# Loading a 2 KB vector in 16 descriptors and spreading it with selecting products, beside a stream of large loads

## The chip, the cores and the metric

The kernel runs on one core of one Trainium2 chip. The metric is the time of one execution on the device in microseconds (us), as the median of several executions. The profile is of a single execution; its span, from the first to the last instruction, is about 1.4 us shorter than the time.

## The reference

One token of decoding. A layer norm of x (1024 values) feeds two branches, whose results are added to x:

```python
x = A_x
xn = _layernorm(x, axis=-1)
return x + _A_ref(xn, A_k_cache, A_v_cache, A_wq, A_wo) + _B_ref(xn, B_w1, B_w2, B_w3, B_w4)
```

Branch A is attention of 32 query heads over 4 heads of K and V with 65,536 cached rows of 128. Branch B is a small network of two gelu layers with the weights w1 to w4. Everything is bf16. The weights are 36 MB and the cache is 134 MB, and each byte is read once: 169.87 MB for 2 KB of output.

## The kernel before

Three large SBUF slots take turns with 8.39 MB each (64 KB in each of 128 partitions): wq, then w1 with w2, then w3, then the eight K blocks (slots 0 and 2) and the eight V blocks (slot 1), then wo and w4. SP issues all of these. x alone is issued by ACT:

```python
_dma(q_act, chan("x"), lambda e: e.dma_start(out=x_bf, in_=A_x[0, 0, :].rearrange("(p j) -> p j", p=P)), writes=[b_x])
kv_load(0, "s0", rows_src(A_wq, 0, 8), 8 * HQD)
...  # w1, w2
kv_load(2, "s2", rows_src(B_w3, 0, 8), 8 * F)
```

A load is issued when its slot has been used up. For the first blocks this ties the loads to the front chain, which starts with x:

```python
_op(q_dve, lambda e: e.tensor_copy(xT, x_bf), reads=[b_x], writes=[b_xT])
...
layer_norm(xT, b_xT, xn, xn_bf, b_xn, 200)
...  # 64 products of xn with wq (slot 0)
issue(3)                                   # K0 into slot 0
...  # w1, w2
issue(4)                                   # V0 into slot 1
...  # w3, gelu -> gh_bf
q_sp.wait_all([(q.sem, q.cnt) for q in (q_pe, q_dve, q_act, q_pool)])
issue(5)                                   # K1 into slot 2
```

After each block m follow `issue(6 + 2 * m)` and `issue(7 + 2 * m)`, the next V and the K after the next. I call the loads K0, V0, K1, V1 and so on. The first instruction of SP and of ACT is moved to the head of the program, ahead of the start-up barrier.

Of the kernel before, what the change touches and what calls it, by code (L numbers as in the profile page):

```python
# [6 lines left out]
BF = mybir.dt.bfloat16  # L7
F32 = mybir.dt.float32
ACTF = mybir.ActivationFunctionType
ALU = mybir.AluOpType  # L10
# [89 lines left out]
def _deps(q, reads, writes):  # L100
    evs = [e for b in reads for e in b.w.items()]
    for b in writes:
        evs += list(b.w.items()) + list(b.r.items())
    q.wait_all(evs, in_order=q.name == "pe")


def _done(ev, reads, writes, partial=False):
    for b in reads:
        b.add_read(ev)
    for b in writes:  # L110
        if partial:
            b.add_write(ev)
        else:
            b.set_write(ev)


def _op(q, fn, reads=(), writes=(), partial=False, loop=False):
    _deps(q, reads, writes)
    ev = q.op(fn, True, loop)
    _done(ev, reads, writes, partial)  # L120
    return ev


def _grp(q, fns, reads=(), writes=(), partial=False):
    _deps(q, reads, writes)
    ev = None
    for i, fn in enumerate(fns):
        ev = q.op(fn, i == len(fns) - 1)
    _done(ev, reads, writes, partial)
    return ev  # L130
# [8 lines left out]
def _dma(q, chan, fn, reads=(), writes=(), partial=False):  # L139
    _deps(q, reads, writes)  # L140
    chan.n += 1
    ev = q.dma(fn, chan.sem, 16 * chan.n)
    _done(ev, reads, writes, partial)
    return ev


def bass_parallel_sum__gqa_block_cached__mixer_s_mlp__decode_kernel(
# [13 lines left out]
    P = 128  # L161
# [6 lines left out]
    KT_D = D // P  # L168
# [10 lines left out]
    with ExitStack() as es:  # L179
        E = es.enter_context  # L180

        def sb(name, shape, dt):
            return E(nc.sbuf_tensor(name, shape, dt))

        def ps(name, shape, dt):
            return E(nc.psum_tensor(name, shape, dt))

        def sem(name):
            return E(nc.semaphore(name))
# [5 lines left out]
        permR = sb("permR", [P, P], BF)  # L195
# [29 lines left out]
        def early(n, dt):  # L225
            size = n * (2 if dt is F32 else 1)
            o = e_off[0]
            e_off[0] = o + (size + 15) // 16 * 16
            assert e_off[0] <= SLOT
            v = KV[:, 2, o:o + size]  # L230
            return v.bitcast(F32) if dt is F32 else v
# [6 lines left out]
        maskA = early(4 * G, F32).rearrange("p (a g) -> p a g", a=4)  # L238
        mD32 = early(32 * 4, BF).rearrange("p (k a) -> p k a", a=4)
        neghalf = early(1, F32)  # L240
        permWE = early(4 * P, BF).rearrange("p (w q) -> p w q", w=4)
        x_bf = early(KT_D, BF)
        xT = early(KT_D, F32)
        xn = early(KT_D, F32)
        xn_bf = early(KT_D, BF)
# [9 lines left out]
        g_bf = early(KT_D, BF)  # L255
# [8 lines left out]
        M_ps = ps("M_ps", [P, 512], F32)  # L264

        _Q.clocks = {}
        q_pe = _Q("pe", sem("c_pe"))
        q_dve = _Q("dve", sem("c_dve"), sem("l_dve"))
        q_act = _Q("act", sem("c_act"), sem("l_act"))
# [4 lines left out]
        def chan(name):  # L274
            if name not in chans:
                chans[name] = _DmaChan(sem("d_" + name))
            return chans[name]

        b_const = _B()
        b_x = _B(); b_xT = _B(); b_xn = _B(); b_xn2 = _B(); b_qT = _B(); b_Y = _B(); b_Yc = _B()  # L280
# [8 lines left out]
        def kv_load(s, ch, src, n, bufs=None):  # L289
            _dma(q_sp, chan(ch), lambda e: e.dma_start(out=KV[:, s, 0:n], in_=src), writes=b_KV[s] if bufs is None else bufs)  # L290

        def rows_src(w, r0, nrow):
            return w.rearrange("(p r) n -> p (r n)", p=P)[:, r0 * w.shape[1]:(r0 + nrow) * w.shape[1]]

        _dma(q_act, chan("x"), lambda e: e.dma_start(out=x_bf, in_=A_x[0, 0, :].rearrange("(p j) -> p j", p=P)), writes=[b_x])
        kv_load(0, "s0", rows_src(A_wq, 0, 8), 8 * HQD)
        b_w1 = b_KV[1][0:2]
        b_w2 = b_KV[1][2:4]
# [15 lines left out]

        evs = []
        for t_, val in ((ident_bf, 0.0), (ident_f[:], 0.0), (ones_f, 1.0), (sel16[:], 1.0), (selGT_bf[0:8, :], 1.0), (selTT[0:4, :], 1.0),
                        (neghalf, -0.5), (permWE, 1.0), (permR[:], 1.0), (maskA, 1.0), (mD32, 1.0), (g_bf, 0.0)):
            evs.append(q_pool.op(lambda e, t_=t_, val=val: e.memset(t_, val)))
        q_pool.wait_all([evs[-1]])

        def sel(t_, pattern, op, base, mult, fill):
            return q_pool.op(lambda e: e.affine_select(out=t_, in_=t_, pattern=pattern, compare_op=op, fill=fill, base=base, channel_multiplier=mult))
# [4 lines left out]
        q_pool.wait_all([ev])  # L327
        sel(sel16[:], [[8, 16]], ALU.is_ge, 7, -1, 0.0)
        sel(selGT_bf[0:8, :], [[0, 16], [-1, 8]], ALU.is_equal, 0, 1, 0.0)
        sel(selTT[0:4, :], [[0, 4], [-1, 4], [0, 8]], ALU.is_equal, 0, 1, 0.0)  # L330
        sel(permWE, [[-64, 2], [-1, 2], [0, 4], [-2, 32]], ALU.is_equal, 0, 1, 0.0)
        sel(permR[:], [[-8, 4], [-32, 4], [-1, 8]], ALU.is_equal, 0, 1, 0.0)
# [3 lines left out]
        ev = sel(maskA, [[32, 4], [0, 8]], ALU.is_ge, 31, -1, 0.0)  # L336
        b_const.set_write(ev)

        _op(q_dve, lambda e: e.tensor_copy(xT, x_bf), reads=[b_x], writes=[b_xT])  # L339

        def layer_norm(src, b_src, dst_f, dst_bf, b_dst, c0):
            _op(q_dve, lambda e: e.reduce_sum(ln_s[:, 0:1], src, axis=AX.X), reads=[b_src], writes=[b_ln])
            _op(q_pe, lambda e: e.matmul(M_ps[:, c0:c0 + 1], ones_f, ln_s[:, 0:1], start=True, stop=True),
                reads=[b_ln, b_const], writes=[b_M])
            _op(q_dve, lambda e: e.tensor_scalar(out=ln_s[:, 1:2], in0=M_ps[:, c0:c0 + 1], scalar1=-1.0 / D, scalar2=None, op0=ALU.mult),
                reads=[b_M], writes=[b_ln])
            _op(q_dve, lambda e: e.tensor_scalar(out=ln_xc, in0=src, scalar1=ln_s[:, 1:2], scalar2=None, op0=ALU.add),
                reads=[b_src, b_ln], writes=[b_ln])
            _op(q_dve, lambda e: e.tensor_tensor(out=ln_sq, in0=ln_xc, in1=ln_xc, op=ALU.mult), reads=[b_ln], writes=[b_ln])
            _op(q_dve, lambda e: e.reduce_sum(ln_s[:, 2:3], ln_sq, axis=AX.X), reads=[b_ln], writes=[b_ln])  # L350
            _op(q_pe, lambda e: e.matmul(M_ps[:, c0 + 1:c0 + 2], ones_f, ln_s[:, 2:3], start=True, stop=True),
                reads=[b_ln, b_const], writes=[b_M])
            _op(q_dve, lambda e: e.tensor_scalar(out=ln_s[:, 3:4], in0=M_ps[:, c0 + 1:c0 + 2], scalar1=1.0 / D, scalar2=EPS,
                                                 op0=ALU.mult, op1=ALU.add), reads=[b_M], writes=[b_ln])
            _op(q_pool, lambda e: e.tensor_tensor(out=ln_s[:, 4:5], in0=ln_s[:, 3:4], in1=neghalf, op=ALU.pow),
                reads=[b_ln, b_const], writes=[b_ln])
            _op(q_dve, lambda e: e.tensor_scalar(out=dst_f, in0=ln_xc, scalar1=ln_s[:, 4:5], scalar2=None, op0=ALU.mult),
                reads=[b_ln], writes=[b_dst])
            _op(q_dve, lambda e: e.tensor_copy(dst_bf, dst_f), reads=[b_dst], writes=[b_dst])  # L359
# [9 lines left out]
            reads=[b_M, b_misc], writes=[b_misc])  # L369
        ev = _op(q_dve, lambda e: e.reduce_sum(maskD[:, :], mD32.rearrange("p k a -> p a k"), axis=AX.X), reads=[b_const], writes=[b_misc])  # L370
        b_const.add_write(ev)

        layer_norm(xT, b_xT, xn, xn_bf, b_xn, 200)

        fns = []
        for j in range(KT_D):
            for jj in range(4):
                for b in range(2):
# [3 lines left out]
                        start=(j == 0), stop=(j == KT_D - 1), tile_position=(0, 32 * jj)))  # L382
# [5 lines left out]
                                                 start=(b + i == 0), stop=True, skip_group_check=True)  # L388
# [4 lines left out]
        for h in range(HKV):  # L393
            for we in range(4):
# [3 lines left out]
                    reads=[b_M, b_const], writes=[b_Y], partial=(h + we > 0))  # L398
# [281 lines left out]
        for hf in range(2):  # L680
            out_halves(27, (hf,), 3 + hf, last=True)
            _op(q_dve, lambda e, hf=hf: e.tensor_tensor(out=orow[:, hf, :], in0=ost[:, 128 * hf:128 * hf + 128], in1=S_ps[:, 2 + hf, 0:128], op=ALU.add),
                reads=[b_ost, b_half[hf]], writes=[b_orow], partial=(hf == 1))
# [93 lines left out]
```

## Time and profile before

| | before |
|---|---|
| time, median (range) of 6 runs | 400.40 us (400.29 to 400.79) |
| span of the profiled run, granted clock | 398.9 us, 0.646 |
| moved from HBM | 169.87 MB by the queue of SP |
| time between the landings of two K blocks | 38.7 us for 16.78 MB |
| K0, V0, K1, V1 issued | 33.12, 51.62, 70.13, 99.49 us |
| K0, V0, K1 landed | 69.4, 88.7, 108.1 us |

Issue times are from the timeline; a landing is the issue time plus the "us to landing" of the view of the transfers, asked for a window that holds only that issue.

### The profile page before, as it was taken

What the parts mean: (1) busy time and instruction counts of PE and PEld (TensorE: products, weight loads), DVE (VectorE), ACT (ScalarE), POOL (GpSimd) and SP (SyncE); (2) the same over time, 40 slices, a digit from 0 to 9 for tenths busy, and PEclk for the clock granted to TensorE, in tenths of its full rate; (3) what the DMA queues carried; (4) which work ended last, traced back from release to release, by engine and by line L of the source; (5) the groups of instructions that cost most, each with busy time, mean ns of one, the idle gap of its engine ahead of it and who ended that gap; (6) DMA issues with size and microseconds to landing.
All of it is one profiled execution on the core that took longest, in us unless ns stands there. A gap on an engine that the chain in (4) does not pass through costs nothing.

```text
span 398.9 us, 3478 instructions
## 1 busy us (share of the span) xinstructions
PE 176.1 (44%) x1555; PEld 59.5 (15%) x1496; DVE 221.9 (56%) x262; ACT 23.9 (6%) x50; POOL 7.7 (2%) x31
## 2 busy tenths in 40 slices
PE   0034767238034723570357036513651462147484
PEld 0011434002001210110012001100120110011232
DVE  0024221994298549833984597269647952895201
ACT  1000000011001100110011002000100110011000
POOL 5000000000000000000000000000000000000000
PEclk9999668556655655576558555655585558555988
DMA  9999899999999999999999999999999999999995
GB/s 421 421 389 491 383 421 493 440 416 427 421 427 429 421 467 440 434 427 421 434 427 421 453 453 434 421 421 427 434 427 427 473 440 421 421 427 427 424 410 234
DMA packets 3907, 169.97 MB, mean 426 GB/s; under 512 B 572, under 2 KB 828, under 8 KB 956
## 3 DMA queue, kind: packets, MB, share of 16 engines
q1 hardware_dynamic: 3756, 169.87, 98.8%
q8 instruction: 5, 0.08, 0.1%
q10 hardware_dynamic: 144, 0.00, 0.0%
q14 instruction: 2, 0.02, 0.0%
HBM read 169.87 MB, written 0.00 MB: 426 GB/s over the span
## 4 chain that ended last, share of the span: by engine, by line
DMA 58%; DVE 25%; PE 13%; issue 1%; ACT 1%; SPq 0%; POOL 0%; DVEq 0%
DMA KV<-in_A_k_cache_dram 45%; DVE KV L460 18%; DMA KV<-in_B_w_dram 8%; DMA KV<-in_A_x_dram 6%; PE S_ps L411 3%; PE OT_ps L518 2%; DVE mrow L481 2%; PE M_ps L426 2%; PE S_ps L474 2%; PE S_ps L379 1%; ACT p_sb L496 1%; DVE Yall L395 1%; DVE pT_f L509 1%; PE PT_ps L505 1%; DVE pT_f L419 1%
## 5 line engine op out<-in xcount | busy, mean ns | idle before, releaser
L460 DVE STREAM_TRANSPOSE KV<-KV 128x4096 f32<-128x4096 f32 x32 | 140.3, 4421 | 43.3 <-DMA KV<-in_A_k_cache_dram 43.3
L474 PE MATMUL S_ps<-KV,Ycur 128*32 128x512 bf16 x512 | 60.7, 623 | 127.2 <-DVE KV L460 127.2
L518 PE MATMUL OT_ps<-KV,pT_f 128*32 128x512 bf16 x512 | 46.7, 506 | 1.0 <-DVE pT_f L509 1.0
L474 PEld LDWEIGHTS S_ps<-KV,Ycur 128*32 128x32 bf16 x512 | 14.3, 126 | 159.2 <-DVE KV L460 141.6
L496 ACT ACTIVATE p_sb<-S_ps,brun 128x1024 bf16<-128x1024 f32 x16 | 17.8, 1114 | 275.8 <-DVE brun L494 175.4
L509 DVE STREAM_TRANSPOSE pT_f<-PT_ps 128x512 f32<-128x512 f32 x32 | 22.5, 702 | 14.0 <-PE PT_ps L505 14.0
L481 DVE TENSOR_REDUCE mrow<-S_ps 128x1 f32<-128x1024 f32 x16 | 19.3, 1206 | 11.3 <-PE S_ps L474 11.3
L484 PE MATMUL M_ps<-Rm,Lmat 128*128 128x16 bf16 x16 | 3.1, 194 | 38.0 <-DVE Rm L482 38.0
L505 PE MATMUL PT_ps<-p_sb,permR 128*128 128x512 bf16 x32 | 18.6, 581 | 0.8
L529 DVE SCALAR_TENSOR_TENSOR O_acc<-O_acc,ff,OT_ps 128x512 f32<-128x512 f32 x12 | 9.0, 748 | 14.6 <-PE OT_ps L518 14.6
L518 PEld LDWEIGHTS OT_ps<-KV,pT_f 128*32 128x32 bf16 x512 | 13.1, 115 | 23.5 <-issue 16.3
L411 PE MATMUL S_ps<-KV 128*32 128x512 bf16 x88 | 12.4, 556 | 2.7 <-DVE KV L359 2.7
L339 DVE CAST KV<-KV 128x8 f32<-128x8 bf16 x1 | 0.2, 172 | 22.2 <-DMA KV<-in_A_x_dram 22.2
L606 PE MATMUL S_ps<-KV,o_bf 128*1 128x512 bf16 x64 | 8.8, 442 | 4.6 <-DMA KV<-in_A_wo_dram 4.6
L484 PEld LDWEIGHTS M_ps<-Rm,Lmat 128*128 128x128 bf16 x16 | 1.7, 104 | 49.3 <-DVE Rm L482 49.3
L426 PE MATMUL M_ps<-ident_f,pT_f 64*128 64x2 f32 (+2 forms) x32 | 7.9, 372 | 2.5 <-DVE pT_f L419 2.5
L426 PEld LDWEIGHTS M_ps<-ident_f,pT_f 64*128 64x128 f32 (+2 forms) x32 | 7.7, 326 | 4.7 <-DVE pT_f L419 3.1
L419 DVE COPY pT_f<-S_ps 64x512 f32<-64x512 f32 (+1 forms) x3 | 2.1, 686 | 11.1 <-PE S_ps L411 11.1
L611 DVE COPY pT_f<-S_ps 1x512 f32<-1x512 f32 x1 | 0.7, 679 | 13.4 <-PE S_ps L606 13.4
L505 PEld LDWEIGHTS PT_ps<-p_sb,permR 128*128 128x128 bf16 x32 | 3.3, 103 | 27.0 <-ACT p_sb L496 14.7
L364 PE MATMUL M_ps<-KV 8*128 8x8 bf16 x1 | 0.2, 182 | 16.0 <-DVE Dmat_f L363 16.0
L672 POOL MEMSET pT_f<- 64x512 f32 x1 | 0.5, 518 | 312.6 <-PE OT_ps L518 312.6
(92 smaller groups left out, 92.4 us busy)
## 6 DMA issues: line engine op xcount, KB each, us to landing
KV<-in_B_w_dram SPq DMA_DIRECT2D x1, 7168.0 KB, 48.0
KV<-in_B_w_dram SPq DMA_DIRECT2D x1, 4352.0 KB, 27.4
KV<-in_B_w_dram SPq DMA_DIRECT2D x2, 2048.0 KB, 28.2
KV<-in_B_w_dram SPq DMA_DIRECT2D x1, 1792.0 KB, 31.3
KV<-in_B_w_dram SPq DMA_DIRECT2D x1, 768.0 KB, 32.8
KV<-in_B_w_dram SPq DMA_DIRECT2D x2, 128.0 KB, 32.6
KV<-in_A_k_cache_dram SPq DMA_DIRECT2D x8, 46.8
KV<-in_A_v_cache_dram SPq DMA_DIRECT2D x8, 28.0
```

Of the source, the lines that this page charges most:

```text
L411: fns.append(lambda e, j=j, k=k, mv=mv: e.matmul(S_ps[32 * (k % 4):32 * (k % 4) + 32, bank + k // 4, :], vec[:, j:j + 1].broadcast_to([P, ...
L419: _op(q_dve, lambda e, b=b, nb=nb: e.tensor_copy(pT_f[0:32 * nb, b, :], S_ps[0:32 * nb, bank + b, :]), reads=[b_S[bank + b]], writes=[b_pT ...
L426: fns.append(lambda e, b=b, nb=nb, c=c: e.matmul(M_ps[:, c0 + 16 * b + c:c0 + 16 * b + 4 * nb:4], pT_f[0:32 * nb, b, c:512:4], ident_f[0:3 ...
L460: _op(q_dve, lambda e: e.transpose(out=KV32[:, s, o:o + 4096], in_=KV32[:, s, o:o + 4096]), reads=[b_KV[s][sub]], writes=[b_KV[s][sub]], l ...
L474: fns.append(lambda e, we=we, cm=cm, mv=mv: e.matmul(S_ps[32 * cm:32 * cm + 32, n % 4, :], Ycur[:, we, :, :].rearrange("p a g -> p (a g)") ...
L481: _op(q_dve, lambda e: e.reduce_max(mrow[:, k:k + 1], S_ps[:, 2 * k:2 * k + 2, :].rearrange("p b c -> p (b c)"), axis=AX.X), reads=b_S[2 * ...
L496: _op(q_act, lambda e: e.activation(p_sb[:, :, :].rearrange("p b c -> p (b c)"), S_ps[:, 2 * k:2 * k + 2, :].rearrange("p b c -> p (b c)") ...
L505: _op(q_pe, lambda e: e.matmul(PT_ps[:, :], permR[:, :], p_sb[:, n % 2, :], start=True, stop=True), reads=[b_p[n % 2], b_const], writes=[b ...
L509: _op(q_dve, lambda e: e.transpose(out=pT_f[:, n % 2, :], in_=PT_ps[:, :]), reads=[b_PT], writes=[b_pT[n % 2]], loop=True)
L518: fns.append(lambda e, q=q, q4=q4: e.matmul(OT_ps[32 * q4:32 * q4 + 32, g % 2, :], pT_bf[:, n % 2, q, :, 1], KV[:, s, 8192 * sub + 512 * q ...
L529: _op(q_dve, lambda e: e.scalar_tensor_tensor(out=O_acc[:, 0:512], in0=O_acc[:, 0:512], scalar=ff[:, k:k + 1], in1=OT_ps[:, k, :], op0=ALU ...
L606: _grp(q_pe, [lambda e, j=j, jj=jj: e.matmul(S_ps[32 * jj:32 * jj + 1, 1, :].rearrange("p (h n) -> p h n", h=2), o_bf[:, j:j + 1], KV[:, 0 ...
```

## The change

x arrived 22 us after its issue, because its eight small descriptors per DMA engine took turns with the eight 64 KB rows of wq. The change loads x as 16 rows of 128 bytes, one per engine, so that it needs fewer turns. x then stands in 16 partitions with 64 values each, and the kernel wants 8 values in each of 128 partitions. Eight products (b = 0 to 7) with a shifted selection matrix, whose row p has its only one in column 8p + b, put the eight values from 8b on of row p into partition 8p + b.

```diff
-        x_bf = early(KT_D, BF)
+        x16 = early(64, BF)
+        selX = early(7 + P, BF)
...
-        _dma(q_act, chan("x"), lambda e: e.dma_start(out=x_bf, in_=A_x[0, 0, :].rearrange("(p j) -> p j", p=P)), writes=[b_x])
+        _dma(q_act, chan("x"), lambda e: e.dma_start(out=x16[0:16, :], in_=A_x[0, 0, :].rearrange("(p j) -> p j", p=16)), writes=[b_x])
...
-                        (neghalf, -0.5), (permWE, 1.0), ...
+                        (neghalf, -0.5), (selX[0:16, :], 0.0), (permWE, 1.0), ...
...
+        sel(selX[0:16, :], [[-1, 7 + P]], ALU.not_equal, 7, 8, 1.0)
...
-        _op(q_dve, lambda e: e.tensor_copy(xT, x_bf), reads=[b_x], writes=[b_xT])
...
+        _grp(q_pe, [lambda e, b=b: e.matmul(M_ps[:, 320:320 + KT_D], selX[0:16, 7 - b:7 - b + P], x16[0:16, 8 * b:8 * b + 8], start=(b == 0), stop=(b == 7)) for b in range(8)],
+             reads=[b_x, b_const], writes=[b_M])
+        _op(q_dve, lambda e: e.tensor_copy(xT, M_ps[:, 320:320 + KT_D]), reads=[b_M], writes=[b_xT])
         layer_norm(xT, b_xT, xn, xn_bf, b_xn, 200)
```

The removed cast stood ahead of DVE's small set-up work, the new products and their evacuation stand behind it.

## The prediction

> **What bounds the kernel now.** I read the page first: the busy shares, the 40 slices, the chain of waits, then the costliest groups.
>
> ```profile
> PE 176.1 (44%) x1555; PEld 59.5 (15%) x1496; DVE 221.9 (56%) x262; ACT 23.9 (6%) x50; POOL 7.7 (2%) x31
> ...
> DMA  9999899999999999999999999999999999999995
> ...
> DMA 58%; DVE 25%; PE 13%; issue 1%; ACT 1%; SPq 0%; POOL 0%; DVEq 0%
> ```
>
> No compute engine is busy for more than 56% of the span of 398.9 us, while the DMA row is full from the first slice to the last but one. That makes the transfers the suspect. The next lines seem to contradict it, because the changed load is both in the chain and in the groups:
>
> ```profile
> DMA KV<-in_A_k_cache_dram 45%; DVE KV L460 18%; DMA KV<-in_B_w_dram 8%; DMA KV<-in_A_x_dram 6%; PE S_ps L411 3%; PE OT_ps L518 2%; DVE mrow L481 2%; PE M_ps L426 2%; PE S_ps L474 2%; PE S_ps L379 1%; ACT p_sb L496 1%; DVE Yall L395 1%; DVE pT_f L509 1%; PE PT_ps L505 1%; DVE pT_f L419 1%
> ...
> L339 DVE CAST KV<-KV 128x8 f32<-128x8 bf16 x1 | 0.2, 172 | 22.2 <-DMA KV<-in_A_x_dram 22.2
> ```
>
> The load of x is 2 KB, takes 22 us and has 6% of the chain. Whether that 6% can be had back depends on what happens where this chain meets the next long transfer, so I read the chain in order of time, and then the times at which the queue of SP issues its loads.
>
> ```profile
> 0.11 22.06 DMA KV<-in_A_x_dram
> ...
> 27.48 5.62 PE S_ps L379 x64
> ...
> 69.92 0.20 DVE gh_bf L439
> 70.13 37.98 DMA KV<-in_A_k_cache_dram
> 108.13 13.10 DVE KV L460 x3
> ```
>
> The columns are start, duration and what. At 70.13 us SP issues the second K block, and it lands 37.98 us later. One block is 8.39 MB. From this landing (108.13) to that of the last K block (340.58, the same view) 12 blocks landed, so one takes 232.45/12 = 19.37 us, which is 433.0 GB/s. So a block that needs 37.98 us was not moving all that time: about half of it, it stood behind another block. The early part of the chain therefore ends in a queue, not in a free DMA engine. The view of the issues, taken for short windows, gives each landing:
>
> ```profile
> KV<-in_A_wq_dram SPq DMA_DIRECT2D x1, 22.0
> KV<-in_A_x_dram ACTq DMA_DIRECT2D x1, 2.0 KB, 22.1
> KV<-in_B_w_dram SPq DMA_DIRECT2D x1, 7168.0 KB, 48.0
> ```
>
> With the issue times of the timeline: wq lands at 22.0, w1 at 0.92+26.0 = 26.9, w2 at 31.8, w3 at 2.14+48.0 = 50.1, K0 (issued 33.12, 36.3 us) at 69.4, V0 (issued 51.62, 37.1 us) at 88.7, K1 at 108.1. So K0 is issued 17.0 us before w3 is in, V0 17.8 us before K0 is in, K1 18.6 us before V0 is in, and V1 (issued 99.49) 8.6 us before K1 is in. The queue always holds more. It is the bytes that bound this kernel: 169.87 MB at 433.0 GB/s are 392.3 us, and the last weights land just before 395.85.
>
> **What the Trainium skill says.** All of it is in "DMA: Bandwidth & Descriptors".
> - "Queues, rings and completion order": each DMA engine takes turns between the queues that have work for it, a packet at a time. This explains how 2 KB can take 22 us, and the trace agrees. The queue of x (q10) has 144 packets, 9 for each of 16 engines: 8 pieces of 16 bytes and, I infer, one for the semaphore. wq gives each engine 8 rows of 64 KB; one x packet after each row means that x ends with wq, and it does, 22.17 against 22.0.
> - "Why a DMA increments its semaphore by 16 and not by 1": the number of engines is the largest one up to 16 that divides the slowest dimension of both sides. 16 rows still give 16 engines, with one data packet each instead of 8. No run shows this yet.
> - "Where 436 GB/s comes from": 16 ports give 435.2 GB/s. The measured 433.0 is 99.5% of it, so there is no spare rate that an earlier start could use.
> - "Specifications": below 512 bytes a transfer does not reach line rate, and does a read-modify-write. 128 bytes is still below; what counts is that there are fewer of them.
>
> **The change part by part.** *Landing of x.* Two packets per engine instead of nine. In before the ninth came after the eighth row of wq, at 22.17. The second should come after the second row, six rows sooner. A row of 64 KB takes 65,536 B/(433.0/16 GB/s) = 2.42 us, so x lands at 22.17 - 6 x 2.42 = 7.6 us (5.2 if its turn comes a row earlier).
>
> *POOL.* One memset and one select more. The timeline has 0.83 us for four small memsets and 0.29 for a 128x128 select, so about 0.5 us in all; the constants are ready at about 7.1 instead of 6.6. That is now in front of x's path, but close to x's own landing.
>
> *PE and DVE.* The eight products (K = 16, 8 columns) are put behind the small set-up on both engines. That set-up took 22.28 to 23.91 in before, 1.6 us. Now it can run from about 7.2 to 9. Eight products by some 0.07 us (four 128x32 products took 0.26) are 0.5 us; with the evacuation, which takes the place of the removed cast at the same 0.17, and two handovers, 0.9 us. The layer norm from its first reduction (23.83) to the start of the products (27.48) is 3.6 us. So xn is ready at about max(9, 7.6) + 0.9 + 3.6 = 13.5 us, some 8 us before wq is in. The added work is all hidden.
>
> *Where the gain goes.* The 64 products of q now wait for wq, at about 22.1, not for the layer norm at 27.48: 5.4 us sooner. The rest follows by the same 5.4 us as long as its weights are in: the first projection at 36.7 (w1 in at 26.9), the second at 42.9 (w2 in at 31.8), the third at 52.7 (w3 in at 50.1, 2.6 us to spare), gh_bf at 64.7. The loads K0, V0 and K1 are issued 5.4 us sooner, at 27.7, 46.2 and 64.7, into a queue that is not empty; they land when they did. The first transpose then waits for K0 (69.4), where it started at 70.12: of 5.4 us, 0.7 are left. With them the first block ends at about 98.8 instead of 99.5, and DVE waits for K1, still due at 108.1. Where DVE waited 7.66 us it will wait 8.4. From there both kernels are the same.
>
> *What is left for the end.* Only DMA time that x itself took. For the first 25 us the view of the queues reads:
>
> ```profile
> q1 hardware_dynamic: 251, 10.14, 96.6%
> q10 hardware_dynamic: 144, 0.00, 0.3%
> ```
>
> 0.3% of 25 us is 0.08 us per engine, and seven of nine packets go: 0.06 us. Gaps around the packets do not count as busy. The fine slices of these 25 us put wq's rows about 2.46 us apart, against 2.42 at the steady rate: 0.04 x 8 = 0.3 us at most, a rough reading. I take 0.2 us. Sum: 400.44 - 0.2 = 400.2 us.
>
> **The rivals.** *The gain of 5.4 us arrives.* For it: x is 6% of the chain, and 22.2 us of DVE's idle time are laid to it; 400.4 would become 395.0 (1.3%). Against it: the queue is full at each of the issues, and the rate is at its ceiling. The whole run cannot move 169.87 MB by 5.4 us sooner without a hole in the DMA row to fill. This stays within 2% as well.
>
> *The small packets disturb more than they are busy.* If each of the eight turns cost a round of latency, wq and everything behind it would land sooner. For it: wq's landing at 22.0 is 2.6 us later than 8 rows of 2.42 (19.4), of which some belongs to the start and the end of any transfer. At most about 1.5 us would come of it: 399.0. Against it: the row spacing of 2.46 us leaves only 0.3.
>
> *The spreading becomes the new wait.* Eight products, an evacuation and 0.5 us of POOL in front of the layer norm cost some 1.5 us. If x landed late in spite of its fewer packets (say still with wq at 22), the products of q would start at 28.4 instead of 27.48, and K0's issue would slip by 1 us, out of 17 us to spare. The time would stay at 400.4 even then.
>
> *Earlier compute disturbs the granted clock.* PE works earlier beside wq's end; if the throttle takes the clock down longer, blocks end later. V1 has 8.6 us to spare and the later pairs some 8, so this too would stay hidden.
>
> **Range and chances.** All ways but two end between 400.0 and 400.5. The three runs of before lie between 400.29 and 400.79, so 0.3 us of noise either side. The disturbance rival, which I give one chance in six, draws the low end down; nothing draws the high end but noise. Predicted 400.2, range 399.4 to 400.9. 2% is 8 us, more than all that the chain of the start could give: within 2% 0.98, faster 0.01, slower 0.01.
>
> **What would show it.** In the profile after: x lands at about 7.6 us, with 32 packets on q10; the products of q start at 22.1, released by wq; K0 is issued at about 27.7 and takes about 41.7 us to land instead of 36.3; the wait of the first transposes turns to K0; K1's transposes start within 0.5 us of 108.1; the blocks behind it land every 19.4 us. I would be wrong if K1's transposes started by 106 or sooner, if a hole of the DMA row was being filled that I took for an artefact of the slices, or if x still landed with wq.

## The result, and the profile after

| | before | after |
|---|---|---|
| time, median of 6 runs | 400.40 us | 400.35 us (400.21 to 400.42) |
| ratio, 95% interval | | 0.9996 (0.9984 to 1.0009) |
| span, granted clock | 398.9 us, 0.646 | 399.0 us, 0.644 |
| x landed | 22.17 us | 7.5 us |
| products of q start | 27.48 | 22.13 |
| K0, V0, K1 issued | 33.12, 51.62, 70.13 | 27.65, 46.15, 64.59 |
| first transpose of K0 | 70.12 | 69.59 |
| V1 issued | 99.49 | 99.45 |
| first transpose of K1 | 108.13 | 108.31 |

A ratio is the mean time of one kernel's runs over the mean of the other's in the same rounds, so it is not quite the ratio of the medians in the table. The change does what it was made for at the front, 14.7 us on the landing of x and 5.4 us on the products of q, and nothing of it is left at K1.

First the page of the changed kernel: the DMA row of the slices, the queue that carries x (packets, MB, share), and the head of the chain by engine.

```profile
DMA  9999899999999999999999999999999999999995
...
q10 hardware_dynamic: 32, 0.00, 0.0%
...
DMA 60%; DVE 25%; PE 12%; ACT 1%; issue 1%; SPq 0%; POOL 0%; DVEq 0%
```

The queue of x has 32 packets instead of 144, two for each engine. The DMA row is the same as that of the kernel before, digit for digit. The transfers' share of the chain has not fallen but risen, from 58% to 60%. The chain in order of time (start, us, what) shows why:

```profile
0.00 22.00 DMA KV<-in_A_wq_dram
22.13 5.50 PE S_ps L383 x64
...
64.59 43.70 DMA KV<-in_A_k_cache_dram
108.31 13.10 DVE KV L464 x3
```

wq has taken the place of x at the head, and the chain after it is 5.5 us earlier up to the issue of K1. That load then takes 43.70 us where it took 37.98. The 5.5 us stand there in full: K1 is issued sooner, and lands when it did.

What DVE waited for in the first 110 us, before (us in total, times, longest):

```profile
DVE KV L339 <- DMA KV<-in_A_x_dram: 22.2, 1, 22.2
...
DVE KV L460 <- DMA KV<-in_A_k_cache_dram: 7.7, 1, 7.7
DVE KV L433 <- PE M_ps L426: 6.2, 2, 4.0
DVE p_sb L385 <- PE S_ps L379: 5.7, 1, 5.7
```

and after:

```profile
DVE p_sb L389 <- PE S_ps L383: 14.4, 1, 14.4
DVE KV L464 <- DMA KV<-in_A_k_cache_dram: 12.8, 2, 7.9
...
DVE Lmat L363 <- PE M_ps L362: 7.3, 1, 7.3
```

The wait of 22.2 us for x is gone. In its place stand 7.3 us for the constants, 8.7 us more for the products of q (14.4 instead of 5.7; these wait for wq), and 5.1 us more for K (12.8 instead of 7.7, and two waits instead of one: K0 is new). Together that is 7.3 + 8.7 + 5.1 = 21.1 us. The waiting changed its name.

The timeline of the changed kernel (start, us, engine, line, what, and in brackets the idle time before it and what ended it) has the two places where this happens:

```profile
13.09 0.17 DVE L360 CAST KV<-KV 128x8 bf16<-128x8 f32 x1
...
22.13 5.46 PE L383 MATMUL S_ps<-KV 128*32 128x512 bf16 x64 [10.18 <-DMA KV<-in_A_wq_dram]
...
69.59 13.10 DVE L464 STREAM_TRANSPOSE KV<-KV 128x4096 f32<-128x4096 f32 x3 [4.92 <-DMA KV<-in_A_k_cache_dram]
```

xn is ready at 13.3 us, and 8.8 us later the products start, with wq. At 64.7 the front chain is done, and DVE stands 4.92 us for K0.

### The profile page after: what moved, and what is told of

Same layout as the page of the kernel before. It is cut to its first block, busy times and chain, and to the rows that moved or that the text cites. A ratio compares the mean times of both kernels' runs of the same rounds, so it can differ in the third digit from the quotient of the medians.

```text
span 399.0 us, 3498 instructions
## 1 busy us (share of the span) xinstructions
PE 176.1 (44%) x1563; PEld 59.2 (15%) x1504; DVE 222.2 (56%) x262; ACT 23.9 (6%) x50; POOL 8.0 (2%) x33
## 4 chain that ended last, share of the span: by engine, by line
DMA 60%; DVE 25%; PE 12%; ACT 1%; issue 1%; SPq 0%; POOL 0%; DVEq 0%
DMA KV<-in_A_k_cache_dram 46%; DVE KV L464 18%; DMA KV<-in_B_w_dram 8%; DMA KV<-in_A_wq_dram 6%; PE S_ps L415 3%; PE OT_ps L522 2%; DVE mrow L485 2%; PE M_ps L430 2%; PE S_ps L478 2%; PE S_ps L383 1%; ACT p_sb L500 1%; DVE Yall L399 1%; DVE pT_f L513 1%; PE PT_ps L509 1%; DVE pT_f L423 1%
## 5 line engine op out<-in xcount | busy, mean ns | idle before, releaser
L415 PE MATMUL S_ps<-KV 128*32 128x512 bf16 x88 | 12.4, 554 | 2.7 <-DVE KV L360 2.7
L383 PE MATMUL S_ps<-KV 128*32 128x512 bf16 x64 | 5.5, 515 | 10.2 <-DMA KV<-in_A_wq_dram 10.2
L615 DVE COPY pT_f<-S_ps 1x512 f32<-1x512 f32 x1 | 0.7, 679 | 14.4 <-PE S_ps L610 14.4
L389 DVE CAST p_sb<-S_ps 128x512 bf16<-128x512 f32 x1 | 0.7, 692 | 14.4 <-PE S_ps L383 14.4
L509 PEld LDWEIGHTS PT_ps<-p_sb,permR 128*128 128x128 bf16 x32 | 3.3, 103 | 27.1 <-ACT p_sb L500 14.7
```

The lines of the kernel that those rows point to most:

```text
L383: fns.append(lambda e, j=j, b=b, jj=jj: e.matmul(S_ps[32 * jj:32 * jj + 32, b, :], xn_bf[:, j:j + 1].broadcast_to([P, 32]), KV[:, 0, j * H ...
L415: fns.append(lambda e, j=j, k=k, mv=mv: e.matmul(S_ps[32 * (k % 4):32 * (k % 4) + 32, bank + k // 4, :], vec[:, j:j + 1].broadcast_to([P, ...
L509: _op(q_pe, lambda e: e.matmul(PT_ps[:, :], permR[:, :], p_sb[:, n % 2, :], start=True, stop=True), reads=[b_p[n % 2], b_const], writes=[b ...
```

## The experiments

All ran against the kernel before on the same chip, in the same rounds, in three batches on three chips. The medians of the kernel before in these rounds were 400.46 to 400.52.

### How much later may x be? late_w1, late_w2, late_w3

The change makes x early and gains nothing. If the queue hides the front chain, x may also be late, up to a slack, and then the end must move one for one. The three runs are the kernel before with the load of x moved into the queue of SP, behind w1, w2 or w3:

```diff
-        _dma(q_act, chan("x"), lambda e: e.dma_start(out=x_bf, ...), writes=[b_x])
         ...
         _dma(q_sp, chan("w2"), ...)
+        _dma(q_sp, chan("x"), lambda e: e.dma_start(out=x_bf, ...), writes=[b_x])   # late_w2; one line up or down for the others
         ...
-        for eng in (nc.sync.engine, nc.scalar.engine):
+        for eng in (nc.sync.engine,):          # ACT has no load to put at the head any more
```

> The kernel before, with its load of x (128 descriptors) queued on SP behind wq and w1, so that x lands about 5 us later (27.3 instead of 22.17) and the whole front chain slips by 5 us. My theory (the queue is full, V1 is issued at 99.5 with K1 landing at 108.1, so a slip of up to about 6 to 7 us costs nothing; the removal of the same 5.4 us gained nothing for the same reason): within 0.5 us of the kernel before, V1 issued at about 104.6. Rival (the front chain is on the path, and the change's gain was lost to something that the change itself added): 5 us longer, 405.5.

> The same with x behind w2, so that x lands about 9.9 us later, at 32. My theory: the slip is over the slack; V1 is issued at about 109.4, after the queue has run dry at about 107, so the transfers lose some 3 to 4 us and the time is 403 to 405. Rival (front chain on the path): 410. If the time is unchanged, the slack is larger than I think.

> The same with x behind w3, so that x lands about 28 us later, at 50.2. My theory: 28 less a slack of 6 to 7 us, so 420 to 424, with two holes in the DMA row: before K0 (issued at about 61, w3 in at 50) and before V1 (issued at about 127, K1 in at about 121). Rival (front chain on the path): 428.

| | before | late_w1 | late_w2 | late_w3 |
|---|---|---|---|---|
| time, median | 400.46 | 401.66 (400.54 to 402.30) | 406.10 (405.07 to 406.91) | 422.90 (422.46 to 424.01) |
| ratio | | 1.0027 (1.0006 to 1.0047) | 1.0139 (1.0118 to 1.0160) | 1.0558 (1.0540 to 1.0575) |
| x landed | 22.17 | 27.1 | 31.8 | 48.8 |
| V1 issued | 99.49 | 105.77 | 110.15 | 127.45 |
| V1 later by | | 6.28 | 10.66 | 27.96 |
| span longer by | | 1.4 | 6.0 | 23.8 |
| slack (V1 later less span longer) | | 4.9 | 4.7 | 4.2 |

V1's issue slipped by the slip of x and, in these runs, by 1.0 to 1.3 us more, of which 0.6 to 0.8 are the products of q: they took 6.2 to 6.4 us instead of 5.6. The end moved by this slip less 4.2 to 4.9 us, over a range of 1.4 to 23.8 us. So the front chain does reach the end, but only with what is over a slack of some 4.5 us. By the medians of the times instead of the single profiled spans the slack is 5.0 to 5.5. My expectations of late_w1 and late_w2 missed here: I had put the slack at 6 to 7 us, so that 5 us would cost nothing, and they cost 1.2; and late_w2 took 406.1 where I had 403 to 405. The rival's 405.5, 410 and 428 are all clearly off.

Where the time goes in late_w2 is seen in the window from 100 to 115 us. The columns are window, length, PE, PEld, DVE, ACT and POOL busy (instructions), granted clock, DMA share and GB/s. Before:

```profile
100.00:115.00 15.00, 1.90 (x16) 0.45 (x16) 7.34 (x4) 0.00 (x0) 0.00 (x0) 0.60 0.99 428
```

and late_w2:

```profile
100.00:115.00 15.00, 8.82 (x84) 2.36 (x84) 9.72 (x14) 1.29 (x3) 0.00 (x0) 0.73 0.71 288
```

The DMA engines were at 0.71 instead of 0.99, which is 0.28 x 15 = 4.2 us lost between the end of K1 and the start of V1. The records of the single packets in the trace are finer. In late_w2 the first engine has no row left at 105.85 us and V1's first rows start at 111.1 to 111.5, a hole of 4.9 us in the mean of the 16 engines; and these first rows take 0.7 us longer than the 2.42 of the others. Together that is 5.6 of the 6.0 us. The same sum gives 1.4 of 1.4 us in late_w1 and 23.0 of 23.8 in late_w3, which has two such holes, one of them before K0, in its row of slices:

```profile
DMA  9999429999929999999999999999999999999995
```

So in these runs the time goes into holes of the DMA engines. The kernel before has none that the front chain could fill: by the same records its engines are idle for 0.4 us in the mean between 1.5 and 393.5 us (the 8 in the row of slices is no hole), and those of the changed kernel as long. The change had nothing to win.

### x alone in front: x_first

```diff
-        _dma(q_act, chan("x"), ...)
+        _dma(q_sp, chan("x"), ...)             # SP's first load, wq is its second
         kv_load(0, "s0", rows_src(A_wq, 0, 8), 8 * HQD)
         ...
-        for eng in (nc.sync.engine, nc.scalar.engine):
+        for eng in (nc.sync.engine,):
```

> The kernel before, with x as SP's first load and wq as its second, so that x lands alone, at about 2 us, with no turns taken with wq; but wq is issued at about 0.9 us instead of 0.0. My theory (the transfers bound the end, the landing of x does not matter): 0.9 us longer, 401.3, though x lands 20 us sooner and the products of q start as soon as wq is in. If x's turns between wq's rows cost transfer time, that comes off: 400.4 to 401.3. Rival (front chain on the path): about 5 us shorter, 395.

x landed at 1.6 us, earlier than in the changed kernel, and wq was issued at 0.79 instead of 0.00. The products of q started at 22.76, K1's transposes at 108.73 instead of 108.13. The time was 401.07 us (400.90 to 401.22), ratio 1.0017 (1.0001 to 1.0034): 0.6 us longer. 20 us on the landing of x bought nothing; 0.79 us on the start of the stream cost most of its own length. wq took 21.83 us to land where it took 22.0 beside the small packets, so at most 0.2 us came back for these.

### What a small packet costs the stream: x_more and x_more2

```diff
+        x_evs = [_dma(q_act, chan("y"), lambda e, c=c: e.dma_start(out=ydump[:, 8 * c:8 * c + 8], in_=A_x[0, 0, :].rearrange("(p j) -> p j", p=P))) for c in range(16)]
         ...
-        q_sp.wait_all([ev_out])
+        q_sp.wait_all([ev_out, x_evs[-1]])
```

> The kernel before with 16 more loads of the same x in the same 128 descriptors behind the first, on the ACT queue, into a scratch tile that nothing reads: 144 small packets more on each DMA engine, one turn after each large row, until about 350 us. It measures what a small packet costs the stream, which bounds what the change saved by having 7 fewer per engine. By the busy share of the small packets in the first 25 us (about 9 ns each per engine): 1.3 us longer, 401.7. By my upper reading of the row spacing (40 ns each): 5.8 us longer, 406. Rival (a small packet costs a round of latency, 0.2 us or more): 29 us or more.

434.12 us, ratio 1.0842. By its number alone this is the rival's result: 33.7 us for 144 packets, 0.23 us each. The trace says otherwise. The timeline of ACT:

```profile
0.92 69.02 ACTq L297 DMA_DIRECT2D ydump<-in_A_x_dram  x16
69.97 1.28 ACT L388 ACT_TABLE_LOAD   x1 [69.97 <-issue]
```

ACT stood in its own 16 issues until 69.9 us. Nine loads of x (the kernel's own and eight of the added) went out by 5.2 us, the next took 18.3 us to issue. ACT's half of the evacuation of q, which belongs at 33 us, came at 71.3, and the front chain with it: V0 was issued at 88.46 and not at 51.62. The run measured a blocked engine, not a packet. What it does show of the packets is that the loads beside them were not held up: wq landed at 21.9 and w3 at 2.12 + 47.4 = 49.5, where it had been 22.0 and 50.1, though 227 records of the small queue fell into the first 25 us instead of 144.

The mended form issues each added load behind one of the 16 exponentials of the blocks (`x_evs.append(_dma(q_act, chan("y"), ...))` at the end of `EXP(g)`), so that they never pile up:

> The mended form of the run with 16 more loads of x: each is issued behind one of the 16 exponentials of the blocks instead of all at once, so that ACT is not held up by its own issues (in the first form it stood until 70 us). Again 144 small packets more on each DMA engine, beside full-rate rows. In the first form wq and w3 landed no later than in the kernel before although the small packets beside them had gone from 144 to 227 in the first 25 us, so the theory that they cost next to nothing says 400.4 to 401.7 (1.3 us is their busy share, if none of it is hidden), rival (0.04 us each) 406, rival (0.2 us each) 429.

The page has all the packets, 144 + 16 x 144 = 2448, and the same DMA row as the kernel before:

```profile
DMA  9999899999999999999999999999999999999995
...
q10 hardware_dynamic: 2448, 0.04, 0.3%
```

The time was 400.64 us (400.49 to 401.75) against 400.52, ratio 1.0014 (1.0000 to 1.0027). By the ratio that is 0.56 us for 144 packets more on each engine, 4 ns each, and at the end of the interval 1.1 us, 8 ns each. The seven packets per engine that the change removes are then worth 0.03 us, 0.05 at most. Both rivals (0.04 us and 0.2 us each) fall.

### The spreading without its gain: spread_late

The changed kernel, with `x16` loaded by SP behind wq instead of by ACT (the same edit as above).

> The changed kernel, with its load of x (16 descriptors) queued on SP behind wq, so that x lands when it did in the kernel before, about 22.3, and the eight products and the longer POOL set-up are paid with no gain. It isolates the cost of the spreading on the front chain. My theory: the products of q start at about 23.1 + 3.6 + 0.3 = 26.8 (the set-up of DVE is done by then, so only products, evacuation and layer norm follow x); the time is that of the kernel before, 400.4 within 0.5. Rival (the added work costs time of its own, which ate a gain): 401 or more.

400.34 us (400.25 to 400.37), ratio 0.9996 (0.9981 to 1.0012). x landed at 22.16, as in the kernel before, and the products of q started at 26.56: not later than 27.48 but 0.9 us sooner. The eight products and their evacuation take about half a microsecond behind x, but DVE's set-up, some 1.6 us that in the kernel before stood behind the cast of x, was done before x came. (The products ran from 22.30 us, and the layer norm's first reduction started at 22.89 instead of 23.83.) The added work cost the end nothing, and the front chain less than the new order saves it.

### Take away the full queue: half_before, half_after, and once more

If the queue hides the 5.4 us, they must appear when it is not full. Both kernels were run with every K and V load but V0 cut to half its bytes; each tile keeps stale data in its other half, so the result is wrong (the check of the result passed these runs all the same), while all compute instructions are the same.

```diff
-                kv_load(slot(i), "v" if isv else "s%d" % slot(i), src, SLOT)
+                t = KV[:, slot(i), :]
+                if i != 4:
+                    src, t = [a.rearrange("p (c k) -> p c k", k=4096)[:, 1::2, :] for a in (src, t)]
+                _dma(q_sp, chan("v" if isv else "s%d" % slot(i)), lambda e: e.dma_start(out=t, in_=src), writes=b_KV[slot(i)])
```

> The kernel before, with every K and V load but the first V cut to half its bytes (the other half of the tile keeps stale data: the result is wrong on purpose; instructions are the same). The transfers then end well before the compute, which becomes the bound: about 352 us. It is the base for the next run.

> The changed kernel with the same cut (wrong result on purpose). My theory (the change's 5.4 us are real, and only the full DMA queue hides them): with the queue no longer full, K0 lands at about 60, before gh_bf at 64.7, nothing absorbs the gain, and this run is 5.4 us, 4.8 to 5.6, shorter than the halved kernel before: about 346.5. Rival (the gain is lost to the added work or to the clock): the two halved kernels agree within 1 us.

347.69 us (347.27 to 349.81) and 343.66 us (343.17 to 344.57), 4.0 us apart; the ratios to the kernel before are 0.8700 and 0.8578. The base was expected at about 352. The gain appears, but as 4.0 us and not 5.4, below the expected 4.8 to 5.6. In these profiled runs the products of q took 5.28 us in the one kernel and 6.58 in the other, which eats 1.3 us. To tell whether that was luck:

> The halved kernel before once more, as the base of the next run: 347.7 as before.

> The halved changed kernel once more, to tell why the first pair differed by 4.0 us and not by 5.4. If the rest was the luck of the granted clock in those runs (its products of q took 6.6 us against 5.3, at 0.54 of the clock against 0.71 between 45 and 60 us), this pair should differ by another amount, around 5.4, and the page should show the products of both at like durations. If products that start sooner always get a lower clock in this stage, the difference is again 3.5 to 4.5 and the products of the changed kernel are again the longer ones.

349.26 us (348.51 to 349.39) and 344.12 us (342.20 to 344.58), 5.1 us apart, on another chip than the first pair; ratios 0.8717 and 0.8586. The chain of the halved kernel before, second time:

```profile
0.12 22.05 DMA KV<-in_A_x_dram
...
27.47 6.09 PE S_ps L382 x64
...
70.97 8.68 DVE KV L463 x2
```

and that of the halved changed kernel:

```profile
0.00 22.04 DMA KV<-in_A_wq_dram
22.18 5.52 PE S_ps L386 x64
...
64.72 13.01 DVE KV L467 x3
```

Now the products are the shorter ones in the changed kernel. The transposes of K0 follow gh_bf at once in both, 6.25 us apart, with no wait for K0 between. In the first pair they had been 3.5 us apart (69.72 and 66.20). So the duration of these products varies from run to run by over a microsecond, in either kernel. It is not the granted clock, as I had supposed before the run: the view by windows shows 1.00 throughout the products of q in all four runs. Their records show groups of four that start 0.43 us apart at first and 0.22 us later; this step comes after 7 and 11 intervals in the two runs of the halved kernel before, and after 14 and 9 in those of the changed one. What sets it, no run here shows. The two pairs lie around the 5.4 us at the transposes of K0 (3.5 and 6.25), but both below it in the medians of the times (4.0 and 5.1); why, stays open. By these the change is worth 4 to 5 us, 1.2 to 1.5%, of a kernel whose queue is not full. It is worth nothing here because this one's queue is full.

No run pointed to a version that beats both kernels: what would have to shrink is the bytes, or the first and the last microseconds of the stream, and the change touches neither. The kernel's text does show bytes that don't reach the result. For a single token the shifts between w1 and w2 in the reference leave only zeros, and the kernel multiplies w2 by a vector of zeros (`g_bf`) and never reads what it makes of w1 (`h1g_bf`). These two weights are 4.19 MB, by my estimate 9.7 us at the measured 433.0 GB/s. No run leaves them out.

## Why the prediction was right, point by point

- **The bound.** The prediction said that the chain's 6% for x end in a queue. The load of K1 shows it directly, 43.70 us to land instead of 37.98, and the late runs and the halved kernels show both sides of it: the end moves one for one when the queue runs dry, and the gain appears when the queue is not full.
- **The landing of x.** 7.6 us predicted, 7.5 measured. The packet records show the turns. In the kernel before, x has on each engine one record of 16 bytes behind each of the eight 64 KB rows of wq, the last at 21.0 to 21.6 us, and then one of 4 bytes; in the changed one it has a record of 128 bytes behind the first row (4.0 to 4.7 us) and one of 4 bytes behind the second (6.4 to 7.2). So 16 rows did use 16 engines, as the prediction took from the Trainium skill ("DMA: Bandwidth & Descriptors", section "Why a DMA increments its semaphore by 16 and not by 1"), and the choice of the second row over the first was right.
- **The added work.** Constants at 7.02 (7.1 predicted), xn at 13.3 (13.5), products of q at 22.13 (22.1): all hidden behind wq.
- **The way of the gain.** K0 issued at 27.65 (27.7) and landing after 41.9 us (41.7), V0 at 46.15 (46.2), K1 at 64.59 (64.7), transposes of K0 at 69.59 behind a wait for K0 (69.4). Each step holds within 0.2 us.
- **What was left behind K0.** Here a size was off. The 0.7 us that should have been left came to 0.5 at the transposes, and to 0.04 at the issue of V1 (99.45 against 99.49; 98.8 predicted). Between 95 and 97 us PE had 0.50 of its clock in the changed kernel and 0.68 in the one before, and from 92 to 100 us it was busy 6.99 us instead of 6.32. That is the fourth rival, the granted clock, in small; one profile of each cannot say whether the change caused it. Nothing hangs on it, since DVE waits for K1 in both.
- **The 0.2 us for x's own DMA time.** This term of the sum was too large. wq landed at 22.0 in both kernels, K1's transposes began 0.2 us later and not sooner, and x_more2 puts the seven packets at 0.03 us. The reading of the row spacing, 2.46 against 2.42 us, which I had called rough, was below what slices of 0.6 us can carry. By the packet records the second to the eighth row of wq start 2.425 us apart in the kernel before and 2.416 in the changed one, 0.06 us over the six steps. The time of 400.35 lies 0.05 below that of before, which is noise.
- **The disturbance rival** (399.0, one chance in six) is refuted by x_more2.
- **The spreading rival** put the products of q at 28.4 if x stayed late; spread_late had them at 26.56. I had added the new work to the old order and overlooked that DVE's set-up moves in front of x. Its verdict, no effect on the time, held.
- **The slack.** The prediction counted 8.6 us from V1's issue to K1's landing as time to spare. About half of it was: the slack was 4.2 to 4.9 us by the profiled spans. The packet records of late_w2 show what the rest is needed for. The first engine was through with K1 2.3 us before K1 had landed (105.85 against 108.2), V1's first row started 1.0 us after its issue (111.1 against 110.15), and the first rows took 0.7 us longer: 4.0 us together. The change made V1 no later, so the result was not touched.

## What to carry to other kernels

A transfer in the chain of waits is worth shortening only if the next long transfer of the chain was waiting for it; compare how long a load takes to land with how long its bytes take to move, and if the first is much longer, an earlier issue only makes the queue longer. Ask of such a change which hole in the DMA row it fills, and test the answer both ways: make the thing later until the time moves, and take the bound away to see the gain. When an added load makes a kernel slower, look whether the issuing engine stood still before you put the time down to the traffic.

## What the Trainium skill lacked or had wrong

- "DMA: Bandwidth & Descriptors", section "Queues, rings and completion order", gives a packet as typically about 9 to 17 descriptors, by which x's eight per engine could have shared one turn. Here every descriptor took a turn of its own, a 16-byte one as well as a 64 KB row: 144 records for 128 descriptors, which alternate with the rows of wq and landed at 22.17 us; 32 records for 16 descriptors landed at 7.5 us.
- The same page, section "Specifications", says that transfers below 512 bytes are not at line rate and do a read-modify-write, but neither it nor the rest of the page gives what they cost a stream of large rows beside them. Here 144 packets of this kind more on each engine cost the kernel 0.56 us by the ratio (interval 0 to 1.1), 4 ns each.
- I found on none of the pages read how many loads one engine may have under way. Here nine loads of 128 descriptors went out from ACT in 5.2 us, the next took 18.3 us, and ACT did nothing else until 69.9 us.
- Nor how long before the landing of one load the next must be issued so that the engines stay busy. In the three late runs it was about 4 us: the 8.6 us between V1's issue and K1's landing in the kernel before, less the slack of 4.2 to 4.9.
